# A chunked RWKV-6 recurrence with a squared-ReLU MLP behind it: the chunk decay moved beside the state update, one cumulative sum from step 5 on, a last tile in two column halves, and a new order of work

## The chip, the cores and the metric

The kernel runs on one core of one Trainium2 chip. The metric is the device time of one execution in microseconds (us). Lower is better. Six runs of the kernel before took 197.55 to 198.88 us, with a median of 198.63 us.

Five engines work at once, each through its own list of instructions in order: TensorE (PE in the profile; its weight loads are PEld), VectorE (DVE), ScalarE (ACT), GpSimd (POOL) and SyncE (SP), which issues all DMA transfers here. TensorE writes only to PSUM, a memory of eight banks, and VectorE or ScalarE read it from there.

## The reference

There are 4 batches, 8 heads, 768 positions and a head width of 48. First a recurrence runs over the positions, once for each batch and head:

```python
for t in range(S):
    cur = einsum('bhd,bhe->bhde', u * k[t], v[t])
    y[t] = einsum('bhd,bhde->bhe', r[t], state + cur)
    state = w[t][..., None] * state + einsum('bhd,bhe->bhde', k[t], v[t])
```

The result is laid out as 3072 tokens of 384 values, x, and goes through two matrices: `h = x @ w_in` (384 to 2048), `g = max(h, 0)**2`, `out = g @ w_out` (2048 to 384). All arrays are float32. The kernel computes the products in bfloat16 with float32 sums.

## The kernel before, in words

**Steps.** A batch's 768 positions are cut into 6 chunks of 128, so there are 24 steps (`NSTEP`), one per batch and chunk, each for all 8 heads at once. Within a chunk the recurrence becomes matrix products. The decay w enters as a logarithm, which is summed along the chunk:

- `lw` (line 154, ScalarE): logarithm of w into one of `NLW = 3` padded buffers.
- `cum` (line 187, PE): sums along the chunk by a product with a triangular matrix into PSUM bank tile `cp`: line 196 without the position itself, for r, and for steps below `V5 = 8` line 198 too, the negated sum with the position itself, for k. In steps whose state is needed later (all but the last chunk of a batch) lines 191 to 195 form in the same bank, in 8 spare columns, the sum over the whole chunk for every head: one matmul that puts -30000 where a column belongs to the other head of a pair, and four matmuls of the logarithms with ones.
- `exp` (line 200, ScalarE): exponentials in place. From step 8 on there is only one sum, and the exponential for k is taken from it with the sign turned (lines 205 and 206). `rw` (ScalarE) and `kw` (GpSimd) then first divide k by w, so that this sum is the right one. Lines 207 to 209 take the exponential of the chunk sums, `a_c`.
- `rd` (line 211, VectorE): r and k times those exponentials, as `rdec`. `tr` (line 217, PE) transposes it with 8 matmuls into bank tile `tr`, `rkt` (VectorE) copies it out, `p` (PE) forms the scores in `cp`, `pm` (VectorE) masks them.
- `su` (line 244, PE): the chunk's own contribution to the state, k^T v, for pairs of heads, in the bank tile `tr` again. `ts` (line 251, VectorE) adds the old state, `sn` (line 259, GpSimd) multiplies by `a_c` and gives the next state.
- `ku`, `qp`, `vq` (GpSimd) and `q` (VectorE) form the term with u. `y` (PE) adds scores times v and r times the state in bank tile `y`, `ysb` (VectorE) adds the u term, `yt` (PE, bank tile `tr`) transposes the sum and `xt` (ScalarE) puts it in x.

The pools behind `cp`, `tr` and `y` (lines 58 to 60) have one buffer each: the next user of such a bank waits until everything that reads it has ended.

**The two layers.** Tokens go in 12 blocks of 256, that is two steps. `m1` (PE, line 300) makes 6 matmuls for 256 of the 2048 columns, and there are 8 such groups in a block. `rl` (ScalarE, line 309) applies the ReLU, `gt` (VectorE, line 317) squares two groups together. `m2` (PE, line 324) multiplies a quarter of the 2048 rows for one half (128 tokens) of the block, 4 matmuls, into one of four banks; after four quarters `os` (ScalarE, line 329) brings the 128 x 384 result to a buffer, and `store` sends it out. The weights arrive as 8 + 8 float32 pieces (`ld:..:I` and `ld:..:O`) and are cast to bfloat16 by `cast`, even pairs on ScalarE and odd pairs on VectorE. A group `m1:i:g` needs piece g of the first matrix, and the quarter q of `m2` the pieces 2q and 2q+1 of the second.

**Fillers.** `warm:n:b` issues n matmuls of 512 columns on zeros. They compute nothing and keep TensorE's clock up while it would wait.

**The order.** All of it is written out by hand in one string, `order`, of 1029 words. `rd:4` is `rd` of step 4, `m2:0:1:2:0` is block 0, half 1, quarter 2, bank 0, and `ld:5:r` is the load of r for step 5. Each engine takes its words in that order and waits at each for its inputs, its buffers and its bank; nothing overtakes. The four loads of a step have 192 KB each, in rows of 192 bytes.

```python
    with tc.manual_schedule(engines={E.PE, E.DVE, E.Activation, E.Pool, E.SP}):
        for word in order.split():
            name, *args = word.split(":")
            run[name](*[int(x) if x.isdigit() else x for x in args])
```

Of the kernel before, what the change touches and what calls it, by code (L numbers as in the profile page):

```python
# [16 lines left out]
def kernel(  # L17
# [15 lines left out]
    C = 128  # L33
# [29 lines left out]
    def bank(b):  # L63
        return ps_mm.tile([C, 512], FP32, name=f"mm{b}")
# [43 lines left out]
    u_row = consts.tile([1, H, D], FP32)  # L108
# [3 lines left out]
    def load_u():  # L112
        nc.sync.dma_start(out=u_row[:], in_=u[None])

    def ub_():
        ps = tiles["ub"] = ps_y_pool.tile([C, H, D], FP32, name="y")
        nc.tensor.matmul(ps[:], ones_row[:], u_row[:], start=True, stop=True)
# [19 lines left out]
    V5 = 8  # L137
    NLW = 3
# [61 lines left out]
    def exp_(s):  # L200
# [6 lines left out]
        if s % NCH < NCH - 1:  # L207
            a_c = tiles["a_c", s] = a_small.tile([C, HP, 2], FP32, name="a_c")
            nc.scalar.activation(a_c[:], cs[:, 0, DM:DM + 2 * HP].rearrange("p (a e) -> p a e", e=2), AF.Exp)  # L209
# [34 lines left out]
    def su_(s):  # L244
        rdec, v_bf = tiles["rdec", s], tiles["v", s]
        ps_su = tiles["su", s] = ps_tr_pool.tile([C, HP, 2, D], FP32, name="tr")
        for p in range(HP):
            nc.tensor.matmul(ps_su[:, p], rdec[:, 1, 2 * p:2 * p + 2, :],  # L248
                             v_bf[:, 2 * p:2 * p + 2, :], start=True, stop=True)

    def ts_(s):
        ps_su = tiles.pop(("su", s))
        ts = tiles["ts", s] = a_mid.tile([C, HP, 2, D], FP32, name="t_state")
        if s % NCH == 0:
            nc.vector.tensor_copy(ts[:], ps_su[:])
        else:
            nc.vector.tensor_add(ts[:], tiles["S", s][:], ps_su[:])  # L257
# [76 lines left out]

    def warm_(n, b):
# [4 lines left out]
    def ld_(n, x):  # L340
        {"i": load_wi, "o": load_wo}.get(x.lower(), lambda g: load_u() if x == "u" else load_step(g, x))(n)

    run = dict(rw=rw_, kw=kw_, lw=lw_, v=v_, cum=cum_, exp=exp_, rd=rd_, tr=tr_, rkt=rkt_, p=p_, pm=pm_, su=su_, ts=ts_,
# [4 lines left out]
        ld:0:w ld:0:r warm:6:0 ld:1:w ld:0:k lw:0 ld:0:u cum:0 ld:0:v warm:4:1 ld:1:v lw:1 ld:1:r exp:0 ub ld:1:k rd:0  # L348
# [103 lines left out]
```

## Time and profile before

| | us |
|---|---|
| median of six runs | 198.63 |
| the profiled execution's own time | 198.88 |
| its span, first to last instruction | 197.1 |
| PE busy | 189.0 (96%) |
| VectorE busy | 145.4 (74%) |
| ScalarE busy | 131.1 (67%) |
| GpSimd busy | 109.1 (55%) |
| share of 16 DMA engines' time used by loads and stores | 66.1% |
| first group of the first layer starts | 26.2 |
| last evacuation (`os`) starts | 193.4 |

The span is cut into 40 slices of 4.93 us in the rows that are shown below, one digit for each: a 9 stands for 90% or more. PEclk is the clock that TensorE was granted, in tenths. A waits row reads: engine and line that waited, what it waited for, total us, how many times, the longest. A chain row reads: start, length, engine, what it wrote, line, how many instructions. Matmul durations in a profile overlap, since they are pipelined, so the distance between two starts says what a group costs.

### The profile page before, as it was taken

The numbers are of one execution on the slowest core, as the hardware profiler recorded it, in microseconds if no ns is written. First come the engines' busy times: TensorE is split into PE (matmuls) and PEld (weight loads), VectorE is DVE, ScalarE is ACT, GpSimd is POOL, SyncE is SP. The second block draws the span as 40 slices with busy tenths as digits, with TensorE's granted clock in tenths as the row PEclk, the third lists the DMA queues.
The fourth block names the chain that finished last, engine by engine and source line by source line (L and its number), as shares of the span: only waits on it lengthen the run. The fifth ranks groups of instructions, "written<-read, shape, count | busy, mean of one in ns | idle before, by whom it ended". The sixth has DMA issues, their size and how long they took to land.

```text
span 197.1 us, 4956 instructions
## 1 busy us (share of the span) xinstructions
PE 189.0 (96%) x1954; PEld 136.7 (69%) x1958; DVE 145.4 (74%) x202; ACT 131.1 (67%) x278; POOL 109.1 (55%) x124
## 2 busy tenths in 40 slices
PE   6899999999899999999999999999999999999992
PEld 2355576776578777678776688877777778778650
DVE  3348997996879979997969876977897885844210
ACT  3615487894689878879974767678776668438221
POOL 6275926026499899693996299430999390010000
PEclk9879999999999999999999999999999999999999
DMA  6999999989999899899998088615730000015013
GB/s 127 216 227 197 299 256 270 327 182 268 211 184 203 196 189 230 171 213 212 228 195 183 3 179 222 141 22 141 151 74 0 3 0 2 3 40 203 0 40 120
DMA packets 108696, 30.20 MB, mean 153 GB/s; under 512 B 100481, under 2 KB 108674, under 8 KB 108674
## 3 DMA queue, kind: packets, MB, share of 16 engines
q1 hardware_dynamic: 108674, 29.89, 66.1%
q8 instruction: 15, 0.25, 0.5%
q14 instruction: 7, 0.06, 0.1%
HBM read 25.17 MB, written 4.72 MB: 152 GB/s over the span
## 4 chain that ended last, share of the span: by engine, by line
PE 79%; DVE 9%; DMA 5%; ACT 2%; issue 2%; SPq 1%; DVEq 0%; ACTq 0%
PE mm L300 27%; PE mm L324 27%; PE tr L222 6%; PE mm L338 4%; PE cp L234 4%; DMA rk_raw<-in_r_dram 3%; DVE gt L317 3%; PE y L269 2%; PE tr L285 2%; PE cp L196 2%; PE tr L248 2%; DMA w_raw<-in_w_dram 2%; DVE rdec_buf L213 2%; PE y L274 2%; DVE pmT L239 1%
## 5 line engine op out<-in xcount | busy, mean ns | idle before, releaser
L300 PE MATMUL mm<-xT,wi_sb 128*128 128x256 bf16 x576 | 72.7, 273 | 0.4 <-DVE wi_sb L104 0.3
L324 PE MATMUL mm<-wo_sb,gt 128*128 128x384 bf16 x384 | 71.6, 326 | 0.0
L309 ACT ACTIVATE rl<-mm 128x512 f16<-128x512 f32 x96 | 55.6, 599 | 19.6 <-PE mm L300 14.8
L300 PEld LDWEIGHTS <-wi_sb 128*128 128x128 bf16 x576 | 54.1, 98 | 10.1 <-DVE wi_sb L104 0.8
L324 PEld LDWEIGHTS <-gt 128*128 128x128 bf16 x384 | 35.8, 98 | 19.0
L317 DVE TENSOR_TENSOR gt<-rl 128x1024 bf16<-128x1024 f16 x48 | 41.6, 883 | 9.7 <-ACT rl L309 9.7
L261 POOL TENSOR_TENSOR S<-t_state,a_c 128x384 bf16<-128x384 f32 x20 | 17.7, 886 | 32.1 <-DVE t_state L257 16.4
L239 DVE TENSOR_TENSOR pmT<-cp,tri_strict 128x1024 bf16<-128x1024 f32 x24 | 29.2, 1219 | 5.7 <-PE cp L234 5.4
L184 POOL TENSOR_TENSOR vq<-v_raw,q 128x384 f32<-128x384 f32 x24 | 22.7, 949 | 16.8 <-DVE q L180 15.4
L172 POOL TENSOR_TENSOR ku<-rk_raw,u_bc 128x384 f32<-128x384 f32 x24 | 25.1, 1048 | 8.3 <-DMA rk_raw<-in_k_dram 4.3
L213 DVE TENSOR_TENSOR rdec_buf<-rk_raw,cp 128x768 bf16<-128x768 f32 x24 | 22.8, 950 | 8.6 <-ACT a_c L209 5.5
L176 POOL TENSOR_TENSOR qprod<-rk_raw,ku 128x384 f32<-128x384 f32 x24 | 25.1, 1050 | 0.5
L226 DVE COPY rkT<-tr 128x1024 bf16<-128x1024 bf16 x24 | 16.5, 688 | 8.8 <-PE tr L222 8.5
L164 POOL TENSOR_TENSOR rk_raw<-rk_raw,rw 128x384 f32<-128x384 f32 x16 | 18.2, 1136 | 5.9 <-ACT rw L160 5.8
L288 ACT COPY xT<-tr 128x384 bf16<-128x384 bf16 x24 | 11.5, 479 | 9.9 <-PE tr L285 9.8
L329 ACT ACTIVATE o_sb<-mm 128x384 f32<-128x384 f32 x24 | 11.6, 491 | 9.7 <-PE mm L324 9.6
L338 PE MATMUL mm<-warm 128*128 128x512 bf16 x52 | 16.5, 435 | 1.5 <-DVE ones L132 1.3
L156 ACT ACTIVATE lw_buf<-w_raw 128x384 bf16<-128x384 f32 x24 | 12.4, 521 | 6.2 <-DMA w_raw<-in_w_dram 6.2
L279 DVE TENSOR_TENSOR y_sb<-vq,y 128x384 bf16<-128x384 f32 x24 | 13.2, 549 | 3.8 <-PE y L274 3.3
L222 PE MATMUL tr<-ident,rdec_buf 128*128 128x128 bf16 x192 | 15.1, 223 | 0.7 <-DVE rdec_buf L213 0.6
L222 PEld LDWEIGHTS <-rdec_buf 128*128 128x128 bf16 x192 | 12.7, 100 | 3.3 <-DVE rdec_buf L213 1.5
L180 DVE TENSOR_REDUCE q<-qprod 128x8 f32<-128x384 f32 x24 | 13.0, 546 | 0.1
(53 smaller groups left out, 179.3 us busy)
## 6 DMA issues: line engine op xcount, KB each, us to landing
w_raw<-in_w_dram SPq DMA_DIRECT2D x24, 192.0 KB, 3.9
rk_raw<-in_r_dram SPq DMA_DIRECT2D x24, 192.0 KB, 3.8
rk_raw<-in_k_dram SPq DMA_DIRECT2D x24, 192.0 KB, 3.8
v_raw<-in_v_dram SPq DMA_DIRECT2D x24, 192.0 KB, 3.8
out_dram<-o_sb SPq DMA_DIRECT2D x24, 192.0 KB, 2.2
w_st<-in_moe_w_in_dram SPq DMA_DIRECT2D x8, 384.0 KB, 5.9
w_st<-in_moe_w_out_dram SPq DMA_DIRECT2D x8, 384.0 KB, 5.6
u_row<-in_u_dram SPq DMA_DIRECT2D x1, 1.5 KB
```

The lines of the kernel that those rows point to most:

```text
L164: nc.gpsimd.tensor_mul(k_s, k_s, tiles.pop(("rw", s))[:])
L172: nc.gpsimd.tensor_mul(ku[:], raw["rk", s][:, 1], u_bc[:])
L176: nc.gpsimd.tensor_mul(qp[:], raw["rk", s][:, 0], tiles.pop(("ku", s))[:])
L184: nc.gpsimd.tensor_mul(vq[:], raw["v", s][:], tiles.pop(("q", s))[:, :, None].to_broadcast([C, H, D]))
L213: nc.vector.tensor_mul(rdec[:, :, :, 0:D], raw["rk", s][:], tiles.pop(("cs", s))[:, :, 0:DM].rearrange("p a (h d) -> p a h d", h=H))
L222: nc.tensor.transpose(ps_tr[:, i, p, :], rdec[:, i, 2 * p:2 * p + 2, :], ident[:])
L239: nc.vector.tensor_mul(pmT[:].rearrange("p e a t -> p (e a) t"), tiles.pop(("p", s))[:].rearrange("p e (a t) -> p (e a) t", a=HP), tri_str ...
L300: nc.tensor.matmul(ps1[:, j * width:(j + 1) * width], wi_sb[:, kk, n * 128:(n + 1) * 128], xT[:, kk, s0 * C:s0 * C + width], start=(kk == ...
L309: nc.scalar.activation(tiles["rl", i, q][:, j], tiles.pop(("m1", i, g))[:], AF.Relu, scale=RS)
L317: nc.vector.tensor_mul(tiles["gt", i][:, 4 * q:4 * q + 4, :].rearrange("p a b -> p (a b)"), rl, rl)
L324: nc.tensor.matmul(tiles["m2", i, mt][:, 0:DM], gt[:, n, mt * 128:(mt + 1) * 128], wo_sb[:, n, :], start=(n == 0), stop=(n == NT - 1))
L338: nc.tensor.matmul(ps[:], warm[:, 0:C], warm[:], start=True, stop=True)
```

## The change

The five matmuls for the chunk sums leave `cum` and follow the state update in `su`, in spare columns of the bank `tr`. A new word, `ac`, takes their exponential there on ScalarE. `V5` becomes 5, so that steps 5, 6 and 7 have one cumulative sum, and get `rw` and `kw`. `NLW` becomes 4. The row of u is loaded into the first row of `u_bc`. A new word, `last`, computes the last 128 tokens of the output as two halves of 192 columns, each with its own bank, evacuation (the first on ScalarE, the second on VectorE) and store. And the whole order is written anew: fillers go from 14 words with 56 matmuls to 16 words with 49, every load is still made once, and the words of each step keep their dependences. Of the order the diff here shows the first rows, to where step 6 is transposed, and the last.

```diff
--- before.py
+++ after.py
@@ -105,16 +105,16 @@
 
     u_bc = consts.tile([C, H, D], FP32)
 
-    u_row = consts.tile([1, H, D], FP32)
+    u_row = u_bc[0:1]
     ones_row = consts.tile([1, C], FP32)
     nc.vector.memset(ones_row[:], 1.0)
 
     def load_u():
-        nc.sync.dma_start(out=u_row[:], in_=u[None])
+        nc.sync.dma_start(out=u_row, in_=u[None])
 
     def ub_():
         ps = tiles["ub"] = ps_y_pool.tile([C, H, D], FP32, name="y")
-        nc.tensor.matmul(ps[:], ones_row[:], u_row[:], start=True, stop=True)
+        nc.tensor.matmul(ps[:], ones_row[:], u_row, start=True, stop=True)
 
     def uc_():
         nc.scalar.copy(u_bc[:], tiles.pop("ub")[:])
@@ -134,8 +134,8 @@
     nc.gpsimd.memset(other_head[:], 0.0)
     nc.gpsimd.memset(other_head[0:DP, :, 1:2], -30000.0)
     nc.gpsimd.memset(other_head[DP:C, :, 0:1], -30000.0)
-    V5 = 8
-    NLW = 3
+    V5 = 5
+    NLW = 4
     lw_bufs = []
     for i in range(NLW):
         t = consts.tile([C, H, DP], BF16, name=f"lw_buf{i}")
@@ -187,12 +187,6 @@
     def cum_(s):
         lw = tiles["lw", s]
         cs = tiles["cs", s] = ps_cp.tile([C, 2, 512], FP32, name="cp")
-        if s % NCH < NCH - 1:
-            nc.tensor.matmul(cs[:, 0, DM:DM + 2 * HP], ident[:], other_head[:], start=True,
-                             stop=False, skip_group_check=True)
-            for p in range(HP):
-                nc.tensor.matmul(cs[:, 0, DM + 2 * p:DM + 2 * p + 2], lw[:, 2 * p:2 * p + 2, :],
-                                 ones2[:], start=False, stop=True, skip_group_check=True)
         nc.tensor.matmul(cs[:, 0, 0:DM], tri_strict[:], lw[:, :, 0:D], start=True, stop=True)
         if s < V5:
             nc.tensor.matmul(cs[:, 1, 0:DM], tri_incl_neg[:], lw[:, :, 0:D], start=True, stop=True)
@@ -204,9 +198,9 @@
         else:
             nc.scalar.activation(cs[:, 1, 0:DM], cs[:, 0, 0:DM], AF.Exp, scale=-1.0)
             nc.scalar.activation(cs[:, 0, 0:DM], cs[:, 0, 0:DM], AF.Exp)
-        if s % NCH < NCH - 1:
-            a_c = tiles["a_c", s] = a_small.tile([C, HP, 2], FP32, name="a_c")
-            nc.scalar.activation(a_c[:], cs[:, 0, DM:DM + 2 * HP].rearrange("p (a e) -> p a e", e=2), AF.Exp)
+    def ac_(s):
+        a_c = tiles["a_c", s] = a_small.tile([C, HP, 2], FP32, name="a_c")
+        nc.scalar.activation(a_c[:], tiles["su", s][:, DM:DM + 2 * HP].rearrange("p (a e) -> p a e", e=2), AF.Exp)
 
     def rd_(s):
         rdec = tiles["rdec", s] = rdec_bufs[s % NRD]
@@ -242,19 +236,24 @@
             tri_strict[:, None, :].to_broadcast([C, 2 * HP, C]))
 
     def su_(s):
-        rdec, v_bf = tiles["rdec", s], tiles["v", s]
-        ps_su = tiles["su", s] = ps_tr_pool.tile([C, HP, 2, D], FP32, name="tr")
+        rdec, v_bf, lw = tiles["rdec", s], tiles["v", s], tiles["lw", s]
+        ps_su = tiles["su", s] = ps_tr_pool.tile([C, 512], FP32, name="tr")
         for p in range(HP):
-            nc.tensor.matmul(ps_su[:, p], rdec[:, 1, 2 * p:2 * p + 2, :],
+            nc.tensor.matmul(ps_su[:, p * 2 * D:(p + 1) * 2 * D], rdec[:, 1, 2 * p:2 * p + 2, :],
                              v_bf[:, 2 * p:2 * p + 2, :], start=True, stop=True)
+        nc.tensor.matmul(ps_su[:, DM:DM + 2 * HP], ident[:], other_head[:], start=True,
+                         stop=False, skip_group_check=True)
+        for p in range(HP):
+            nc.tensor.matmul(ps_su[:, DM + 2 * p:DM + 2 * p + 2], lw[:, 2 * p:2 * p + 2, :],
+                             ones2[:], start=False, stop=True, skip_group_check=True)
 
     def ts_(s):
-        ps_su = tiles.pop(("su", s))
+        ps_su = tiles.pop(("su", s))[:, 0:DM].rearrange("p (a e d) -> p a e d", a=HP, e=2)
         ts = tiles["ts", s] = a_mid.tile([C, HP, 2, D], FP32, name="t_state")
         if s % NCH == 0:
-            nc.vector.tensor_copy(ts[:], ps_su[:])
+            nc.vector.tensor_copy(ts[:], ps_su)
         else:
-            nc.vector.tensor_add(ts[:], tiles["S", s][:], ps_su[:])
+            nc.vector.tensor_add(ts[:], tiles["S", s][:], ps_su)
 
     def sn_(s):
         S = tiles["S", s + 1] = a_mid.tile([C, HP, 2, D], BF16, name="S", bufs=3)
@@ -332,6 +331,19 @@
         t0 = (blocks[i][0] + mt) * C
         nc.sync.dma_start(out=out[t0:t0 + C, :], in_=tiles.pop(("o", i, mt))[:])
 
+    def last_(i, mt, b, j):
+        gt, cols = tiles["gt", i], slice(j * DM // 2, (j + 1) * DM // 2)
+        ps, o_sb = bank(b), o_pool.tile([C, DM], FP32, name="o_sb")
+        for n in range(NT):
+            nc.tensor.matmul(ps[:, 0:DM // 2], gt[:, n, mt * 128:(mt + 1) * 128], wo_sb[:, n, cols],
+                             start=(n == 0), stop=(n == NT - 1))
+        if j == 0:
+            nc.scalar.activation(o_sb[:, cols], ps[:, 0:DM // 2], AF.Copy, scale=1.0 / (RS * RS))
+        else:
+            nc.vector.tensor_scalar_mul(o_sb[:, cols], ps[:, 0:DM // 2], 1.0 / (RS * RS))
+        t0 = (blocks[i][0] + mt) * C
+        nc.sync.dma_start(out=out[t0:t0 + C, cols], in_=o_sb[:, cols])
+
     def warm_(n, b):
         ps = bank(b)
         for _ in range(n):
@@ -340,79 +352,79 @@
     def ld_(n, x):
         {"i": load_wi, "o": load_wo}.get(x.lower(), lambda g: load_u() if x == "u" else load_step(g, x))(n)
 
-    run = dict(rw=rw_, kw=kw_, lw=lw_, v=v_, cum=cum_, exp=exp_, rd=rd_, tr=tr_, rkt=rkt_, p=p_, pm=pm_, su=su_, ts=ts_,
+    run = dict(rw=rw_, kw=kw_, ac=ac_, last=last_, lw=lw_, v=v_, cum=cum_, exp=exp_, rd=rd_, tr=tr_, rkt=rkt_, p=p_, pm=pm_, su=su_, ts=ts_,
                sn=sn_, y=y_, ysb=ysb_, yt=yt_, xt=xt_, ku=ku_, qp=qp_, q=q_, vq=vq_, cast=cast, m1=m1_,
                rl=rl_, gt=gt_, m2=m2_, os=os_, store=store, ld=ld_, warm=warm_, ub=ub_, uc=uc_)
 
     order = """
-        ld:0:w ld:0:r warm:6:0 ld:1:w ld:0:k lw:0 ld:0:u cum:0 ld:0:v warm:4:1 ld:1:v lw:1 ld:1:r exp:0 ub ld:1:k rd:0
-        warm:1:2 uc ld:2:w cum:1 v:0 ku:0 exp:1 su:0 ld:3:w warm:3:3 ts:0 v:1 tr:0 sn:0 ld:2:v warm:9:0 rd:1 ku:1 ld:2:r
-        rkt:0 qp:0 lw:2 ld:2:k p:0 qp:1 tr:1 pm:0 ld:0:I warm:4:1 ld:3:r ld:4:w rkt:1 cum:2 y:0 exp:2 su:1 ld:3:k
-        warm:10:2 ts:1 v:2 q:1 sn:1 rd:2 ku:2 ld:3:v q:0 cast:i:0:0 p:1 su:2 vq:0 pm:1 warm:5:3 lw:3 ld:1:I ld:2:I qp:2
-        ld:3:I ts:2 cum:3 ld:4:I ysb:0 vq:1 tr:2 exp:3 ld:4:r y:1 rkt:2 ku:3 ld:4:v warm:1:0 rd:3 yt:0 warm:3:1 xt:0
-        qp:3 ysb:1 lw:4 tr:3 sn:2 v:3 p:2 rkt:3 warm:2:2 pm:2 yt:1 ld:5:I warm:4:3 xt:1 cast:i:0:1 cast:i:1:0 p:3 ld:6:I
-        y:2 q:2 m1:0:0:0 pm:3 vq:2 ld:4:k cast:i:2:0 m1:0:2:1 su:3 rl:0:0 ld:5:w ysb:2 m1:0:4:2 ts:3 v:4 cum:4 q:3
-        ld:7:I yt:2 rl:0:4 m1:0:1:3 vq:3 exp:4 y:3 ld:0:O sn:3 warm:3:0 ysb:3 ld:1:O xt:2 cast:i:1:1 rl:0:2 ld:2:O yt:3
-        warm:1:2 ld:3:O m1:0:3:0 xt:3 rd:4 ku:4 ld:6:w cast:i:2:1 m1:1:4:2 ld:4:O qp:4 rl:0:1 su:4 ld:5:k m1:1:5:1 lw:5
-        gt:0:0 m1:0:5:3 rl:0:3 ts:4 rl:1:4 m1:1:2:0 gt:0:1 rl:1:5 m1:1:0:2 cast:i:3:1 rl:0:5 tr:4 cast:i:3:0 rl:1:2
-        m1:1:3:1 rkt:4 ld:5:r cast:o:0:1 m1:0:6:3 gt:0:2 p:4 rl:1:3 m1:1:1:0 cast:o:1:0 rl:1:0 m1:1:6:1 pm:4 rl:1:1
-        ld:5:O m1:1:7:2 cast:o:0:0 ld:6:O gt:1:2 y:4 lw:6 ld:7:O m1:0:7:0 gt:1:0 rl:0:6 cum:5 gt:1:1 rl:0:7 ld:6:k
-        m2:0:0:0:3 exp:5 cast:o:1:1 m2:0:1:0:0 ld:6:r q:4 rl:1:6 m2:0:0:1:3 vq:4 rd:5 cast:o:2:0 m2:0:1:1:0 ld:5:v ku:5
-        m2:1:1:0:1 m2:1:1:1:1 gt:0:3 cast:o:2:1 sn:4 tr:5 cum:6 qp:5 rkt:5 m2:0:1:2:0 exp:6 cast:o:3:0 m2:0:0:2:3 ld:7:w
-        cast:o:3:1 rl:1:7 m2:1:1:2:1 ku:6 q:5 ld:6:v m2:0:0:3:3 rd:6 m2:0:1:3:0 ld:7:k os:0:0 ysb:4 vq:5 tr:6 ld:7:r p:5
-        rkt:6 m2:1:0:0:2 qp:6 lw:7 ld:7:v pm:5 yt:4 v:5 m2:1:0:1:2 os:0:1 ld:8:w xt:4 gt:1:3 cum:7 v:6 y:5 q:6 ld:8:k
...
-        m1:11:3:2 m2:10:1:2:1 rl:11:3 m2:11:0:0:3 os:10:0 gt:11:1 m2:10:1:3:1 store:10:0 m2:11:1:0:2 m2:11:0:1:3
-        m2:11:0:2:3 m2:11:0:3:3 m2:11:1:1:2 os:11:0 m2:11:1:2:2 os:10:1 store:10:1 m2:11:1:3:2 store:11:0 os:11:1
-        store:11:1
+        ld:0:w ld:0:r warm:6:0 ld:0:k ld:0:u ld:1:w lw:0 ld:1:r cum:0 warm:2:1 ld:1:k exp:0 ub rd:0 ld:0:v lw:1 ld:0:I
+        ld:2:w cum:1 tr:0 ld:1:v exp:1 warm:8:2 rkt:0 uc ld:3:w rd:1 ku:0 v:0 tr:1 ku:1 p:0 rkt:1 warm:2:3 ld:2:v qp:0
+        pm:0 su:0 warm:3:0 ld:2:r ac:0 qp:1 ts:0 v:1 p:1 ld:2:k y:0 lw:2 q:0 su:1 sn:0 warm:6:1 cast:i:0:0 ld:3:k pm:1
+        vq:0 ac:1 ld:3:r q:1 cum:2 warm:5:2 ysb:0 exp:2 vq:1 ld:1:I ld:2:I ts:1 v:2 ld:4:w rd:2 yt:0 sn:1 y:1 lw:3
+        warm:1:3 xt:0 ld:3:v ku:2 ysb:1 cum:3 su:2 warm:4:0 ac:2 qp:2 ld:3:I exp:3 ts:2 yt:1 warm:2:1 rd:3 ku:3 xt:1
+        ld:5:w tr:2 cast:i:0:1 m1:0:0:2 ld:4:I sn:2 rkt:2 cast:i:1:0 warm:1:3 ld:4:r q:2 p:2 lw:4 m1:0:1:0 pm:2 vq:2 v:3
+        tr:3 ld:5:I rl:0:0 qp:3 warm:1:1 rl:0:1 rkt:3 y:2 ld:4:k cast:i:1:1 su:3 lw:5 m1:0:2:3 ysb:2 ld:6:I ac:3 rw:5
+        m1:0:3:1 q:3 ld:5:k p:3 ts:3 vq:3 cast:i:2:0 pm:3 yt:2 warm:1:2 sn:3 ld:7:I rl:0:2 m1:0:4:0 xt:2 gt:0:0 y:3
+        ld:4:v rl:0:3 cum:4 ysb:3 warm:2:2 exp:4 ku:4 yt:3 ld:5:r warm:4:3 xt:3 cast:i:2:1 qp:4 rl:0:4 ld:0:O rd:4
+        m1:0:5:1 ld:1:O ku:5 rl:0:5 cum:5 ld:5:v m1:1:0:2 exp:5 gt:0:1 m1:1:2:3 ld:2:O kw:5 q:4 m1:1:1:0 rl:1:0 ld:3:O
+        gt:0:2 cast:i:3:0 tr:4 ld:4:O vq:4 m1:1:4:1 rd:5 ld:6:w rl:1:1 qp:5 m1:1:6:2 v:4 rkt:4 m1:0:6:0 rl:1:4
+        cast:i:3:1 p:4 rl:1:6 su:4 gt:1:0 ld:6:k m1:1:7:1 cast:o:0:0 pm:4 m1:0:7:2 rl:1:7 ld:5:O ac:4 m1:1:5:1 gt:1:3
+        rl:0:6 ld:6:O y:4 rl:0:7 ts:4 warm:1:0 cast:o:0:1 rl:1:2 tr:5 ld:7:O q:5 v:5 m2:1:1:0:0 cast:o:1:0 rkt:5 ld:7:w
+        vq:5 m2:0:1:0:2 ysb:4 rl:1:5 p:5 ld:7:k cast:o:1:1 yt:4 lw:6 m1:1:3:3 ku:6 pm:5 xt:4 ld:6:r m2:0:1:1:2 rw:6 sn:4
+        m2:0:0:0:1 cast:o:2:0 cum:6 cast:o:2:1 y:5 exp:6 kw:6 m2:0:0:1:1 ysb:5 m2:0:0:2:1 cast:o:3:0 gt:0:3 ld:8:w yt:5
+        m2:0:1:2:2 cast:o:3:1 rl:1:3 ld:7:r gt:1:2 m2:0:0:3:1 xt:5 lw:7 m2:0:1:3:2 ku:7 ld:8:k os:0:0 m1:2:2:3 rw:7 rd:6
+        qp:6 ld:6:v m1:2:3:1 os:0:1 lw:8 gt:1:1 cum:7 ld:8:r tr:6 kw:7 exp:7 m1:2:4:2 rkt:6 ld:7:v m2:1:1:1:0 qp:7 rw:8
...
+        m2:10:1:0:0 rl:11:0 m1:11:1:3 rl:11:2 m1:11:3:2 m2:10:0:0:1 rl:11:3 m2:10:1:1:0 rl:11:1 gt:11:1 m2:10:1:2:0
+        gt:11:3 m2:10:0:1:1 gt:11:0 m2:10:0:2:1 m2:10:1:3:0 m2:10:0:3:1 os:10:1 m2:11:0:0:2 os:10:0 m2:11:0:1:2
+        m2:11:0:2:2 m2:11:0:3:2 os:11:0 store:11:0 store:10:1 store:9:1 store:10:0 last:11:1:3:0 last:11:1:0:1
```

## The prediction, made before the change was run

> **What bounds the kernel now.** I read the page first: busy shares, the forty slices, the waits.
>
> ```profile
> PE 189.0 (96%) x1954; PEld 136.7 (69%) x1958; DVE 145.4 (74%) x202; ACT 131.1 (67%) x278; POOL 109.1 (55%) x124
> PE   6899999999899999999999999999999999999992
> PEclk9879999999999999999999999999999999999999
> DMA  6999999989999899899998088615730000015013
> ```
>
> TensorE (PE) is busy throughout and next to nothing else is idle for it. But the DMA row is full too, for about the first 100 us, so in that stretch data can set the pace. Busy time doesn't separate these, so I took the distance between the starts of neighbouring PE groups, and the chain that ended last shows the same lengths:
>
> ```profile
> 50.59 0.62 PE tr L222 x8
> ...
> 68.11 0.45 PE tr L222 x8
> 68.56 0.65 PE mm L300 x6
> 69.21 0.65 PE mm L324 x4
> ```
>
> Undisturbed, a first-layer group (L300, x6) costs 0.655, a second-layer group (L324, x4) 0.650, a transpose group (L222, x8) 0.447, scores (L234, x8) 0.330, an output group (L269+L274) 0.372 or 0.204 without state, a state update (L248, x4) 0.170, a decay group (L191 + 4 of L194) 0.127, one cumulative sum (L196 or L198) 0.163, a y transpose (L285, x3) 0.167, the u broadcast 0.84. Sum of needed work: 96x0.655 + 96x0.650 + 24x0.447 + 24x0.330 + 20x0.372 + 4x0.204 + 20x0.170 + 20x0.127 + 32x0.163 + 24x0.167 + 0.84 = 168.2 us. The last matmul starts near 193.2, so about 25.0 us of PE time are lost: warm-up fillers and waits. "Lost" at a moment = clock minus needed work issued so far; it never falls. It stands at 18.7 when the first L300 group starts (26.21), 20.3 at 31.80, 20.75 from 38 to 49, 21.55 when `tr:6` starts (50.59), 22.0 at 58, 25.0 at the end. So three quarters is gone before the first-layer work, and the last large step is this one:
>
> ```profile
> 43.74 5.71 DMA rk_raw<-in_r_dram
> 49.57 0.97 DVE rdec_buf L213
> 50.59 0.62 PE tr L222 x8
> ```
>
> The r rows of step 6 land at 49.45, `rd:6` takes 0.97 behind them, and `tr:6` is released. Data are the limit there. The 3.45 us lost later are many small pieces, some 1.6 of it 0.1 at each of sixteen switches to the 64-row score matmuls.
>
> **What the Trainium skill says.** "DMA: Bandwidth & Descriptors", Specifications, wants 512 B or more per transfer for line rate; step loads have 192 B rows. The trace agrees: a 192 B packet takes 15.5 ns and a 1536 B one 72.6, that is 12 against 21 B per ns; by the trace's landing marks a step load (192 KB) costs 0.96 us (17 landings from 47.68 to 64.04), a first-layer weight piece (384 KB) about 1.6 and a second-layer piece 1.24. "PSUM — Partial Sum Buffer", PSUM bank collisions raise a hardware error, tells to guard by bank, two readers on different engines included. The trace agrees: rdec waits for the a_c exponential although it doesn't use it, only because both read bank cp:
>
> ```profile
> DVE rdec_buf L213 <- ACT a_c L209: 5.5, 2, 4.3
> ```
>
> "TensorE: Matmul & The Clock Gate", The HAM clock gate, halves the clock after an idle window of about 3.4 us. Here the granted clock is 0.9 from 3 to 20 us and full afterwards; none of the waits that I find below is that long.
>
> **The change, part by part.**
>
> *Decay sums moved to the state update.* The 5 matmuls (0.127) stay, 20 times; PE work is unchanged. In front of rdec goes the 0.178 us exponential and 0.127 of PE: about 0.3 us off a step's chain, hidden behind other PE work except at the start. Added: `ts` now shares its bank with `ac` and comes after it in the order, so VectorE (in order: then gt, rd, rkt) waits for ScalarE's place in its queue, and bank tr comes free later. The next user of bank tr stands at least 1.9 us of PE work behind the state update from step 3 on (0.2 to 4 before), and the ScalarE work ahead of `ac` is nearly all fed by matmuls before the update: cost 0. If ScalarE lags by 1 us, each update costs 0 to 0.5: bound 0 to +4 us.
>
> *One cumulative sum from step 5.* Three L198 matmuls go: -0.49 us. Added: 3 rw (0.525) and three second exponentials (0.48+0.48 against 0.80) on ScalarE, 2.1 us, and 3 k divisions (1.136) on GpSimd, 3.4 us, between 25 and 55 us. A stretch of that time (columns: stretch, its length, busy PE, PEld, DVE, ACT, POOL, clock, DMA share, GB/s):
>
> ```profile
> 36.00:44.00 8.00, 8.00 (x84) 6.12 (x82) 7.88 (x13) 7.20 (x13) 1.09 (x2) 1.00 0.94 251
> ```
>
> GpSimd has the room; ScalarE has 0.8 of 8 us, and VectorE nearly none. Cost on the path 0, because PE waits for data in that stretch anyway; without that cover up to +1.
>
> *Four lw buffers, u in u_bc.* One memset more (0.53) on GpSimd before 5 us, where its first multiply waits 3.8 us anyway: 0.
>
> *Last tile in halves.* 32 matmuls of 192 columns replace 16 of 384. An L324 matmul of 384 columns takes 0.163, one of L300 with 256 columns 0.109, both 0.425 ns per column; at that rate 32x192 columns cost 2.6, as 16x384 do. The evacuation at the end is half as wide, on VectorE: 0.55 for 384 columns (the t_state row), so some 0.35, against 0.49 on ScalarE: -0.14. The last store has half the bytes: eight packets per engine at 72.6 ns were 0.58 us, so -0.25 at most; but four full stores stand right ahead in SP's order behind `os:11:0`, which ends 2.1 us before the last matmul, and stores spaced 0.5 apart in this trace still landed within 2.1 to 2.15. The last then issues at about +0.42 and lands near +2.1, against +2.36 now. Together -0.3 (0 to -0.5).
>
> *Order, the start.* I walk each engine's queue with the durations above, an operation starting when its inputs, its bank and its engine are free. Loads land about 0.95 apart from 3.6 on: k0 5.4, w1 6.4, v0 9.1. `exp:0` no longer sits behind `lw:1`: it starts with cum:0's end, 5.1 instead of 6.12. Then rd:0 6.0 to 6.9 (0.95), cum:1 behind lw:1 and bank cp 7.05, tr:0 7.5, rkt:0 8.1 to 8.8, rd:1 to 9.75, and after eight fillers tr:1 at 9.8 (13.91 before). p:0 10.4, pm:0 11.2 to 12.4, which frees cp for p:1, y:0 12.9. VectorE then runs ts:0, q:0, pm:1, q:1, ysb:0, ts:1, rd:2 back to back until 17.4 (0.55 each, 1.22, 0.95), y:1 is at 16.8, ysb:1 ends 18.0, ts:2 18.9, yt:1 19.0, xt:1 19.3 to 19.8, tr:2, and the first L300 group starts near 20.3 instead of 26.21. But the weight pieces land as late as before (about 27, 29.5, 32, 34.5 for the fifth to eighth), so PE takes a group now and then: by m1:0:5 (31.6 after cast i:2:1 on ScalarE, 12.0 us of work issued) lost is 19.5, against 20.3. The fillers fall from 56 to 49, which is part of this same 0.8.
>
> *Order, 36 to 54 us.* Here I follow SP's queue. r of step 5 is the 23rd step load, behind eight weight pieces: eight pieces and 21 step loads had landed at 34.86, so it lands at 36.7. `rd:5` stands in front of `rkt:4` on VectorE and holds it: 36.7 + 0.95 + 0.69 gives rkt:4 at 38.4, and PE's `p:4` (17.2 us of work) waits for it: lost 21.2. Behind rkt:4 queue cast i:3:1, gt:1:0, pm:4, gt:1:3, ts:4 (0.94+0.69+1.22+0.69+0.55), which release y:4 and tr:5: lost 22.3 at 42.5. The last second-layer piece comes after 26 step loads (24 before, landing 47.68): 49.6, its cast 0.55, so m2:0:0:3 (27.0) starts at 50.2: lost 23.1. r of step 6 comes after v5, w7 and k7, which it used to precede: 49.45 + 3x0.96 = 52.3; rd:6 until 53.3; tr:6 (29.8 us of work) at 53.4: lost 23.6 against 21.55, **+2.0 us**. Bounds: the DMA share fell to 0.79 from 42 to 46; if the new order closes that gap, 0.8 less; a cast one ScalarE slot late adds 0.6. After that the order has slack: step loads from 7 on arrive 0.8 us or more before PE asks, and from step 9 over 2 us. The later 3.45 I keep (2 to 4.5).
>
> Sum against the profiled execution: +2.0 - 0.5 - 0.3 = +1.2, span 197.1 to 198.3. That execution's time was 198.88, 1.8 outside its span; the median of the runs is 198.63, so I predict 198.63 + 1.2 = 199.8.
>
> **Rivals.** *Faster, 197.1:* the early lead of 0.8 holds, and r6 is not the limit; with -0.5 and -0.3 that is -1.6. For it: tr:1 four us earlier, seven fillers fewer. It decides if r6 lands before about 50.5, two step loads sooner than I count. Against it: the DMA is full to 40 us in both orders. *No change, 198.6:* the DMA gap at 42 to 46 closes (-0.8) and later small waits shrink by 0.5, since state updates have more room in bank tr. For it: the waits ahead of y:8 and tr:10 cost 0.4 together today, that ahead of p:12 0.3. *Worse, 201.8:* ac holds bank tr and VectorE; 20 updates at 0.1 to 0.15 us add 2 to the +1.2. It decides from a ScalarE lag of 2 us behind the matmuls. Against it: in the ten-microsecond stretches after 100 us ScalarE is busy 4.0 to 8.1 of 10. That the decay move does nothing for PE is part of my sum.
>
> **Numbers.** Forecast 0.55, its own range 199.3 to 201.0; worse 0.12; no change 0.20; faster 0.13. A measurement of this kernel can tell about 0.3% (0.6 us) from no change. Slower 0.67, same 0.20, faster 0.13. The range 198.2 to 201.6 leaves out most of the faster case and half of the worse.
>
> **What would show it.** First L300 group at 20 to 21.5; a VectorE wait of some 2 us for r of step 5 near 36.7 and p:4 at 38.4; tr:6 near 53.4 behind `rd:6` and a DMA landing near 52.3; then PE dense to about 194.6; GpSimd busy 3.9 us more and ScalarE 1.9; the last store landing within 2.2 us of the last matmul. I am wrong if tr:6 starts before 51.7, or if ts waits on ac pile up after 60 us.

## The result, and the profile after

The changed kernel takes 200.39 us (median of 29 runs), beside 198.73 us for the kernel before (66 runs). The ratio is 1.0065, with a 95% interval from 1.0046 to 1.0083: 1.3 us slower (0.0065 x 198.7). A ratio here counts only the executions within 1.5% of the quickest of the same kernel (20 of 30 for the changed kernel), so where this matters the text also gives the ratio of the means of all executions, which is 1.0079 for the changed kernel (1.6 us, with an error of 0.4). The prediction was 199.8, in the range 198.2 to 201.6. The profiled execution is one of the quicker ones: 199.48 us, span 197.5, against 198.88 and 197.1 before.

The page of the kernel after, with the busy times and the slices that answer to those shown of before (it has no row for the clock, since this trace holds no record of it):

```profile
PE 185.9 (94%) x1960; PEld 135.9 (69%) x1964; DVE 145.2 (74%) x203; ACT 131.6 (67%) x284; POOL 111.7 (57%) x128
...
PE   7896888988899999999999999999999999999993
DMA  6998999989999999999929972495300100203005
```

PE has work of 167.7 us instead of 168.2, is busy 3.1 us less (fewer fillers, and faster ones, see the last section), and ends later: the last matmul ends at 194.5, 193.3 before. Behind its first slice the DMA row stands at 8 or 9 tenths to about 99 us (20 slices of 4.94 us), as it did before.

The chain that ended last, of the kernel after, answers to the one shown of before (start, length, what):

```profile
51.95 0.96 DVE rdec_buf L207
52.91 0.04 issue
52.95 0.32 PE cp L190
53.28 0.45 PE tr L216 x8
53.72 0.65 PE mm L299 x6
```

The r rows of step 6 were issued at 46.63 and landed 5.2 us later, at 51.83 (49.45 before):

```profile
46.63 2.43 SPq L67 DMA_DIRECT2D rk_raw<-in_r_dram  x1
```

```profile
rk_raw<-in_r_dram SPq DMA_DIRECT2D x1, 192.0 KB, 5.2
```

The product with the decay started 0.12 us after that, as it did in `before`, `r6_late` and `r6_early`, where the profile names these rows as what ended its wait, and PE's next cumulative sum and transpose waited for its end. Here the profile names an evacuation on ScalarE instead:

```profile
DVE rdec_buf L207 <- ACT o_sb L328: 1.5, 1, 1.5
```

That evacuation ended at 51.85, next to the landing, but the product does not use it. The late rows are the step on which the prediction put 2.0 us.

I use the prediction's "lost" again: the time in the trace minus the needed PE work issued so far. One row per trace, at five amounts of issued work; 8 us is about where the first L299/L300 group starts, 14 is past the group `m1:0:5` (after) or `m1:0:3` (before), 30 past `tr:6`:

```
                  8       14      30      36      end of PE
before          18.67   20.33   21.66   21.94   25.16
r6_late         17.60   20.51   24.19   24.48   27.22
tail_alone      17.66   19.58   20.75   21.04   24.58
few_before      17.60   19.27   19.47   19.76   22.49
tail_decay      18.05   20.45   21.37   21.67   28.40
after           15.82   20.02   23.31   23.40   26.77
r6_early        16.41   20.35   21.43   22.17   25.75
r6_sn4          16.54   21.12   22.89   23.67   27.00
r6_cast         15.95   19.39   23.77   24.53   28.05
v5_back         15.94   20.08   23.65   23.76   26.65
few_after       16.22   20.17   21.55   21.64   23.98
decay_back      17.46   21.70   25.17   25.37   29.57
decay_back2     15.52   20.22   23.59   23.80   27.12
```

The last two rows are one and the same kernel: single executions differ by up to 2.5 us, so a row shows where time goes, and the timed ratios say how much. In the two rows that matter most, `before` and `after`: the new order is 2.85 us ahead at 8 (1.6 just behind it, since a wait of 1.2 us follows there), 0.3 ahead at 14, and 1.65 behind at 30. From there to the end both lose the same, 3.46 and 3.50.

### The profile page after: what moved, and what is told of

Read it like the earlier page. It is cut to its first block, busy times and chain, and to the rows that moved or that the text cites. A ratio compares the mean times of both kernels' runs of the same rounds, so it can differ in the third digit from the quotient of the medians.

```text
span 197.5 us, 4952 instructions
## 1 busy us (share of the span) xinstructions
PE 185.9 (94%) x1960; PEld 135.9 (69%) x1964; DVE 145.2 (74%) x203; ACT 131.6 (67%) x284; POOL 111.7 (57%) x128
## 4 chain that ended last, share of the span: by engine, by line
PE 61%; SPq 13%; DMA 9%; DVE 6%; ACT 5%; issue 4%; DVEq 0%; ACTq 0%
PE mm L299 24%; PE mm L323 23%; SPq L67 10%; DMA w_raw<-in_w_dram 4%; PE tr L216 3%; DMA w_st<-in_moe_w_in_dram 3%; PE cp L228 2%; DMA v_raw<-in_v_dram 2%; ACT rl L308 2%; PE cp L190 2%; PE y L268 2%; SPq L332 1%; PE tr L284 1%; PE mm L338 1%; DVE pmT L233 1%
## 5 line engine op out<-in xcount | busy, mean ns | idle before, releaser
L299 PE MATMUL mm<-xT,wi_sb 128*128 128x256 bf16 x576 | 74.0, 273 | 0.9 <-ACT wi_sb L104 0.4
L323 PE MATMUL mm<-wo_sb,gt 128*128 128x384 bf16 x368 | 70.1, 326 | 0.0
L299 PEld LDWEIGHTS <-wi_sb 128*128 128x128 bf16 x576 | 53.7, 98 | 11.2 <-ACT wi_sb L104 1.3
L323 PEld LDWEIGHTS <-gt 128*128 128x128 bf16 x368 | 33.9, 98 | 17.9 <-issue 0.8
L172 POOL TENSOR_TENSOR ku<-rk_raw,u_bc 128x384 f32<-128x384 f32 x24 | 24.2, 1011 | 13.7 <-DMA rk_raw<-in_k_dram 9.1
L184 POOL TENSOR_TENSOR vq<-v_raw,q 128x384 f32<-128x384 f32 x24 | 21.5, 903 | 18.4 <-DVE q L180 18.4
L176 POOL TENSOR_TENSOR qprod<-rk_raw,ku 128x384 f32<-128x384 f32 x24 | 26.2, 1095 | 3.3 <-DMA rk_raw<-in_r_dram 2.8
L164 POOL TENSOR_TENSOR rk_raw<-rk_raw,rw 128x384 f32<-128x384 f32 x19 | 21.5, 1132 | 11.3 <-ACT rw L160 10.5
L168 ACT CAST v_bf<-v_raw 128x384 bf16<-128x384 f32 x24 | 12.3, 512 | 3.9 <-DMA v_raw<-in_v_dram 3.8
L350 PE MATMUL mm<-warm 128*128 128x512 bf16 x45 | 13.5, 416 | 1.4 <-DVE warm L129 1.3
L216 PE MATMUL tr<-ident,rdec_buf 128*128 128x128 bf16 x192 | 14.6, 219 | 0.1
```

Source lines behind the costliest of these rows:

```text
L164: nc.gpsimd.tensor_mul(k_s, k_s, tiles.pop(("rw", s))[:])
L172: nc.gpsimd.tensor_mul(ku[:], raw["rk", s][:, 1], u_bc[:])
L176: nc.gpsimd.tensor_mul(qp[:], raw["rk", s][:, 0], tiles.pop(("ku", s))[:])
L184: nc.gpsimd.tensor_mul(vq[:], raw["v", s][:], tiles.pop(("q", s))[:, :, None].to_broadcast([C, H, D]))
L216: nc.tensor.transpose(ps_tr[:, i, p, :], rdec[:, i, 2 * p:2 * p + 2, :], ident[:])
L299: nc.tensor.matmul(ps1[:, j * width:(j + 1) * width], wi_sb[:, kk, n * 128:(n + 1) * 128], xT[:, kk, s0 * C:s0 * C + width], start=(kk == ...
```

## The experiments

### Late r rows in the kernel before, and few weight loads in both

In `r6_late` the kernel before loads the r rows of step 6 three places later, and nothing else is changed:

```diff
-... m2:0:1:0:0 ld:6:r q:4 ...
+... m2:0:1:0:0 q:4 ...
-... ld:6:v m2:0:0:3:3 ...
+... ld:6:v ld:6:r m2:0:0:3:3 ...
```

> The kernel before with one word moved: the load of r for step 6 goes behind three other step loads (v5, w7, v6) on SP. If data set the pace there, r6 lands some 2.9 us later (near 52.3), the transpose of step 6 starts near 53.4 instead of 50.59, and the time grows by 2.4 to 2.8 us, to about 201.2. If PE has other work to hide it, or the wait is absorbed later, it grows by less than 0.5.

Measured: ratio to before 1.0158 (1.0112 to 1.0203), 3.1 us slower. The chain of this run:

```profile
48.30 3.69 DMA rk_raw<-in_r_dram
...
52.11 0.97 DVE rdec_buf L213
...
53.12 0.62 PE tr L222 x8
```

`tr:6` starts at 53.1, as in the changed kernel, and lost goes from 21.2 to 24.2 there. So this one load, in this place, sets the pace of PE in the old order. The 3.1 us agree, within the interval, with the 2.4 to 2.8 that the data theory asked for.

In `few_before` and `few_after` 14 of the 16 weight pieces are not loaded, and all casts read the first piece of their matrix, so that the output is that of other weights, while the work of PE, VectorE, ScalarE and GpSimd stays the same.

```diff
     def load_wi(h):
+        if h:
+            return
     def load_wo(h):
+        if h:
+            return
-        copy(dst, w_st.pop((kind, h))[:])
+        copy(dst, w_st[kind, 0][:])
```

> The kernel before, with 14 of the 16 weight pieces not loaded (every cast reads the first piece of its matrix, so the two layers compute with wrong weights); all casts and matmuls stay. It takes some 20 us of DMA time away before 50 us. Theory (data set the pace up to 54 us): the wait for r6 and the filler time near 30 us go, 1 to 2 us less than before, 197.2. It is the base for its counterpart.

> The changed kernel with the same 14 weight pieces not loaded. Theory: its loss lies in data that come late in the first 54 us, so without it it is no longer slower: 0.5 to 1.5 us faster than the kernel before with the same loads left out, some 196. Rival (ScalarE's decay exponential holds bank tr and VectorE, or the added ScalarE and GpSimd work): it stays 1 us or more slower than that one.

Measured, against before: 0.9886 (0.9842 to 0.993) and 0.9918 (0.988 to 0.9957). `few_before` is 2.3 us faster than the kernel before, where 1 to 2 were expected. `few_before` loses 0.2 us between 14 and 30 instead of 1.3: PE's waits in that stretch were for data. `few_after` loses 1.4 there instead of 3.3, so some 1.9 us of what the changed kernel lost there was late data as well. But the kernel before loses 1.1 us there to late data too. So of the 2.0 us that the new order loses more than the old one between 14 and 30, the pair of traces puts 0.8 down to late data, and 1.2 stay, 0.6 of them where a second-layer group waits for VectorE's squares (at 48.44 in `few_after`).

I had expected `few_after` to be 0.5 to 1.5 us faster than `few_before`, and it is not: at 0.9918 over 0.9886 it is 0.6 us slower, with an error of 1.2. The rival, that the order costs 1 us or more without late data too, is therefore not excluded. And the early lead, 1.4 us at 8, has become 0.9 us behind by 14, with hardly a weight load in the way, so late weights are not what eats the lead.

The largest part of what eats it stands in the timeline of the changed kernel (start, length, engine, work, and the idle time before it with what ended it):

```profile
30.76 0.48 ACT L287 COPY xT<-tr 128x384 bf16<-128x384 bf16 x1
31.14 0.83 ACT L104 CAST wi_sb<-w_st 128x768 bf16<-128x768 f32 x1
```

```profile
30.56 1.03 PE L350 MATMUL mm<-warm 128*128 128x512 bf16 x4
32.03 0.83 PE L299 MATMUL mm<-xT,wi_sb 128*128 128x256 bf16 x6 [0.44 <-ACT wi_sb L104]
```

The cast that `m1:0:5` needs is queued on ScalarE behind the exponential of step 4 and the copy of y of step 3, though its piece landed at 29.6; and four fillers stand in front of `m1:0:5`. Together 1.48 us are lost there, and 1.46 in `few_after`. That is 1.5 of the 4.2 us that the changed kernel loses between 8 and 14. Another 1.2 go right behind 8, where the output group of step 2 waits for its masked scores, which VectorE makes behind a weight cast; the rest are smaller waits and fillers.

### The loads, a state and a cast put earlier in the changed kernel

```diff
 r6_early
-... ld:7:k ... ld:6:r ... ku:7 ... qp:6 ...
+... ld:6:r ld:7:k ... qp:6 ku:7 ...
 r6_sn4, on top of r6_early
-... ku:6 ... sn:4 ...
+... sn:4 ku:6 ...
 r6_cast, on top of r6_early
-... exp:4 ... xt:3 cast:i:2:1 ...
+... cast:i:2:1 exp:4 ... xt:3 ...
```

`r6_early` takes the product `qp:6`, which needs these rows, ahead of `ku:7` on GpSimd too.

> The changed kernel with the r rows of step 6 loaded one place earlier (ahead of k of step 7). Data theory: r of step 6 lands near 51.1 instead of 51.95, its product with the decay no longer holds the cumulative sum of step 7, and the 0.76 us lost there goes: 0.5 to 0.8 us faster than the changed kernel, ratio to before 1.0025 to 1.004. Rival, engine order: the wait moves to the next thing on PE and nothing is gained, ratio 1.0065.

Measured: 1.0035 (1.0004 to 1.0066), 0.6 us faster than the changed kernel with an error of 0.7. The means of all executions give 1.0074 (error 0.003), beside 1.0079. So the gain that the data theory asked for is not shown by the times. In the trace VectorE takes the product when the rows are there, at 49.61, and PE no longer waits at `tr:6`:

```profile
49.61 0.95 DVE L207 TENSOR_TENSOR rdec_buf<-rk_raw,cp 128x768 bf16<-128x768 f32 x1 [0.27 <-DMA rk_raw<-in_r_dram]
```

That is earlier than the 51.1 expected, because all loads came earlier in this execution (the last second-layer piece at 48.15 instead of 49.28).

`r6_sn4` goes for a wait that the prediction did not have. In the changed kernel the output group of step 5 stood for 0.71 us for the state, which GpSimd made late, since the bonus product of step 6 stands ahead of it in GpSimd's order and waits for k rows (landing 45.27):

```profile
45.34 1.00 POOL L172 TENSOR_TENSOR ku<-rk_raw,u_bc 128x384 f32<-128x384 f32 x1 [3.06 <-DMA rk_raw<-in_k_dram]
46.29 0.83 POOL L260 TENSOR_TENSOR S<-t_state,a_c 128x384 bf16<-128x384 f32 x1
```

```profile
47.18 0.33 PE L273 MATMUL y<-S,rkT 128*128 128x96 bf16 x4 [0.71 <-POOL S L260]
```

> As the run before, and the new state of step 4 is computed on GpSimd ahead of the bonus product of step 6, which waits for k of step 6. Data theory: the 0.87 us wait of the output group of step 5 goes, but the last second-layer piece, which lands near 49.4 and is cast by 50.0, holds PE to the same clock: 0.5 to 1.0 us faster than the changed kernel, ratio 1.0015 to 1.004, no more than 0.3 better than the run before. Rival, the two waits are independent: both sums come in, 1.6 us faster, ratio 0.9985.

Measured: 1.005 (1.0012 to 1.0089). The wait is gone from the trace (lost does not move between 23 and 27 us of work), and the time is no better than that of `r6_early` (over all executions 1.0073, beside 1.0074). The rival's 0.9985 is outside the interval. So taking away this PE wait, which stood ahead of a later wait for data, bought nothing that can be measured here.

> The changed kernel with the r rows of step 6 loaded one place earlier (alone: ratio 1.0035), and the cast of the sixth first-layer piece on ScalarE ahead of the exponential of step 4 instead of behind the copy of y of step 3. Engine-order theory: m1:0:5 starts near 30.9 instead of 32.0 to 32.4, so the 1.48 us lost there shrinks to 0.2 to 0.5. Data theory for the rest: the scores of step 4 and m2:0:0:3 stand where r of step 5 and the last second-layer piece land, so next to nothing of it is left by 50 us: ratio 1.002 to 1.0045. Rival: the gain is kept to the end, 1.0 to 1.3 us, ratio 0.997 to 0.9985.

Measured: 0.9998 (0.9964 to 1.0032), which looks as if the two moves together took back the loss. But this rests on 8 of 22 executions. The means of all, 199.42 and 198.05 us, give 1.0069 (error 0.003), beside 1.0079 for the changed kernel: 0.2 us, with an error of 0.7. So no gain is shown. The smaller ratio touches both expected ranges; that of all executions lies above both, nearer to the data theory's. In its trace, an execution of 200.81 us, the cast is ready at 30.2 and `m1:0:5` starts at 31.41, not 30.9: what is left, 0.86, are the four fillers. The 0.6 won there is gone by the end of the second layer's first block, where `m2:0:0:3` and `m2:0:1:3` wait for the last two second-layer pieces (lost grows by 1.85; the cast of the last piece starts at 50.51).

### The tail alone

```diff
-... m2:11:1:0:2 ... m2:11:1:3:2 ... os:11:1 store:11:1
+... last:11:1:2:0 last:11:1:0:1
```

This is put into the kernel before, with the new function `last_`; the rest is as it was.

> The kernel before with only the last 128 tokens in two column halves; its stores stay where they were. Theory of the prediction: 0.3 us less (0 to 0.5). If the two traces are right, in which 3.7 us lay between the last matmul and the end before and 3.0 after, 0.7 less: 198.0.

Measured: 0.9987 (0.9965 to 1.0009), 0.26 us faster, which can't be told from nothing. From the last matmul's end to the landing of the last store it is 2.05 us in its trace, 2.39 before and 2.06 in the changed kernel; to the span's end 3.46, 3.74 and 3.04. The last evacuation and stores of the changed kernel are

```profile
194.27 0.94 SPq L345 DMA_DIRECT2D out_dram<-o_sb  x2
194.50 0.36 DVE L343 TENSOR_SCALAR o_sb<-mm 128x192 f32<-128x192 f32 x1 [7.27 <-PE mm L338]
```

The 0.36 was forecast as 0.35.

### One cumulative sum undone

```diff
-    V5 = 5
+    V5 = 8
-... rw:5 ... kw:5 ... rw:6 ... kw:6 ... rw:7 ... kw:7 ...
```

> The changed kernel with two cumulative sums again for steps 5 to 7, and without their ScalarE and GpSimd work. Prediction's step: the three matmuls cost 0.49 us, but those of steps 5 and 6 stand where PE waits for data, so 0.16 to 0.5 us slower than the changed kernel, ratio 1.007 to 1.009. Rival: the ScalarE and GpSimd work of the one-sum form costs more in that stretch than the matmuls save, and undoing it gives 0.5 to 1 us: ratio 1.0015 to 1.004.

Measured: 1.0054 (1.0032 to 1.0077), 0.2 us faster than the changed kernel, with an error of 0.6 (over all executions 1.0058, beside 1.0079). Neither the gain that the prediction counted nor a cost shows. PE has 0.49 us more to do and ends at 194.83 instead of 194.46, in one execution of each.

### The decay sums, in both orders

`decay_back` is the changed kernel with the sums and their exponential back in the bank of the cumulative sum; `decay_back2` is the same kernel again.

```diff
     def su_(s):
-        nc.tensor.matmul(ps_su[:, DM:DM + 2 * HP], ident[:], other_head[:], ...)
-        for p in range(HP):
-            nc.tensor.matmul(ps_su[:, DM + 2 * p:DM + 2 * p + 2], lw[:, 2 * p:2 * p + 2, :], ones2[:], ...)
     def cum_(s):
+        if s % NCH < NCH - 1:
+            ... the same five matmuls, into cs[:, 0, ...]
-... su:0 ... ac:0 ...
+... exp:0 ac:0 ... su:0 ...
```

> The changed kernel with the decay sums and their exponential back beside the cumulative sum (its bank, its place). Prediction's theory: the move costs and gains nothing, so within 0.6 us of the changed kernel, ratio 1.0035 to 1.0095. Rival a: the new wait of VectorE's state sum for the decay exponential costs PE time, and undoing it gives 0.6 us or more, ratio under 1.0035. Rival b: the move pays, since it takes 0.3 us off each step's chain, and undoing it costs 0.6 us or more, ratio over 1.0095.

> A second measurement of the changed kernel with the decay sums back beside the cumulative sum. If undoing the move costs time: ratio 1.010 to 1.016 again, and in the trace the r and k product waits for the decay exponential in at least four steps. If the first measurement was chance: ratio 1.005 to 1.009, within the changed kernel's own interval.

Measured: 1.0132 (1.0079 to 1.0184) in 6 runs, then 1.0079 (1.0054 to 1.0104) in 22. The first was mostly chance. Weighted by their errors they give about 1.009, so undoing the move costs 0.5 us, with an error of 0.6: in the new order it is worth 0 to 1 us, which is no more than the error.

`tail_decay` makes the same move in the kernel before, in its own order, together with the tail in halves: 20 times the decay exponential `ac:s` comes right ahead of `ts:s`, with its sums in `su_`. Since the sums now read the logarithms later, it has five log buffers, and two words of step 19 stand further back; the row of u sits in `u_bc`, as in the change. `old_order` made the move too, with four log buffers, `ac:s` right behind `su:s`, the one-sum form for steps 5 to 7 and the tail in halves; my placing of its words spoiled it.

```diff
-    NLW = 3
+    NLW = 5
-... su:14 ... ts:14 ...
+... su:14 lw:19 rw:19 ... ac:14 ts:14 ...
```

The words of `old_order`, for one of the steps:

```diff
-... lw:7 ... rd:7 ... ku:7 ... su:7 ... ts:7 ...
+... lw:7 rw:7 ... ku:7 kw:7 rd:7 ... su:7 ac:7 ... ts:7 ...
```

> All code of the change (decay sums beside the state update, one cumulative sum from step 5 on, four buffers, last tile in halves) in the engine order of before; only the words that the code needs are put in, next to their neighbours. Prediction's theory: the loss lies in the order alone, so tail 0.3 and one-sum 0.2 to 0.5 come in: 0.5 to 0.8 us faster than before, ratio 0.996 to 0.9975. Rival: the code itself costs (ScalarE and GpSimd work in a stretch where they have little room, the state sum behind the decay exponential), ratio over 1.001.

> The kernel before in its own order, with the last tile in halves (alone: ratio 0.9987) and the decay sums moved to the state update, their exponential right ahead of the state sum in the list; five lw buffers, and the logarithm of step 19 moved behind the state update of step 14, since the sums read it later. Prediction's theory, the move is worth nothing: ratio 0.9975 to 1.0005. Rival, the move pays wherever it is made, as undoing it in the changed kernel cost 1.3 us: ratio 0.992 to 0.996.

Measured: `old_order` 1.0324 (1.0277 to 1.0371), `tail_decay` 1.0144 (1.0093 to 1.0195). In `old_order` four log buffers are too few, so that the sums of steps 14 and 15 read the logs of steps 18 and 19; and GpSimd, with `ku:7` and `kw:7` behind `vq:6`, held `rd:7` for nearly 2.0 us. So it says little of the change itself. It does show what the place right behind the state update costs: ScalarE waited there 14.6 us, in 17 waits.

`tail_decay` is the telling one. With the tail alone at 0.9987, the move costs 3.1 us here (0.0157 x 198.7), with an error of about 1.1. Up to 36 us of work it runs like the kernel before, and then loses 6.7 us to the end instead of 3.2. The waits of `tail_decay`:

```profile
DVE t_state L256 <- ACT a_c L203: 8.9, 11, 1.8
...
DVE t_state L254 <- ACT a_c L203: 5.3, 3, 2.2
...
PE tr L216 <- DVE t_state L256: 1.4, 3, 0.8
...
PE tr L216 <- DVE t_state L254: 0.9, 2, 0.6
```

And of the changed kernel:

```profile
ACT a_c L203 <- PE tr L247: 5.8, 7, 2.3
...
DVE t_state L256 <- ACT a_c L203: 2.8, 4, 1.6
```

The state sum shares its bank with the decay exponential and waits for ScalarE: 14.2 us in 14 waits in the old order, 2.8 us in 4 in the new. While it waits, VectorE does nothing else and the bank stays taken, so the next transpose is late, for instance at `tr:12` and `tr:16`:

```profile
94.21 0.56 DVE L254 COPY t_state<-tr 128x384 f32<-128x384 f32 x1 [1.54 <-ACT a_c L203]
...
116.58 0.55 DVE L256 TENSOR_TENSOR t_state<-S,tr 128x384 f32<-128x384 bf16 x1 [1.85 <-ACT a_c L203]
```

The second is in part my own doing: the logarithm of step 19, moved behind `su:14`, stands ahead of that exponential on ScalarE. PE lost 0.96 there; the other 2 us or so have nothing to do with it. So the mechanism of the rival "worse" is real. In the new order it hardly acts; that this comes from the room behind each update, and not from the place of the exponential in ScalarE's list, is argued and was not tested apart.

## Why the prediction was right, and where its steps were not

**The late r rows (+2.0).** Right in place and time: `tr:6` was to start at 53.4 with 23.6 lost, behind rows landing near 52.3. It started at 53.1, lost stood at 23.3, and the rows landed at 51.83. `r6_late` shows that rows as late as this cost the kernel before 3.1 us.

How much of the changed kernel's loss they are is not shown. By the trace PE lost 0.76 us there, of which the profile shows 0.60 as idle time:

```profile
52.95 0.32 PE L190 MATMUL cp<-lw_buf,tri_strict 128*128 128x384 bf16 x1 [0.60 <-DVE rdec_buf L207]
```

The kernel before lost 0.80 for its own rows of step 6. When these waits began, the new order was already 1.8 us behind (lost 22.54 beside 20.74). Most of that had gone between 43 and 48 us, at the scores and the output group of step 5; had PE come sooner, it would have waited longer for the rows. So two limits lie close together, and taking away one of them (`r6_early`, `r6_sn4`) gave no gain clear of the scatter.

**The start.** The first L299 group was to start near 20.3, and started at 21.44. The chain of small steps kept to the forecast up to `y:0` (12.4, forecast 12.9). Then VectorE stood still 1.9 us for the k rows of step 2, which landed at 17.28:

```profile
17.40 0.95 DVE L207 TENSOR_TENSOR rdec_buf<-rk_raw,cp 128x768 bf16<-128x768 f32 x1 [1.92 <-DMA rk_raw<-in_k_dram]
```

The prediction had VectorE busy without a break there. The lead was to shrink to 0.8 by `m1:0:5` because of late weights. It shrank to 0.3, and the largest single cause was another: the cast behind two other ScalarE operations, and four fillers. The prediction had that cast ending at 31.6 "on ScalarE" (it ended at 31.97), but ascribed the loss to the weights; `few_after` shows it with hardly a weight load left.

**The scores of step 4 (lost 21.2).** This step failed in the profiled execution. r of step 5 was counted to land at 36.7 and landed at 35.57, so `p:4` started at 37.3 with 20.1 lost. In the other traces of this order it was in part seen: r of step 5 landed between 34.74 and 38.08, and 0.25 to 0.8 us were lost at `p:4` in five of them. The wait is there when the rows land later than in the profiled execution, or when PE comes sooner (`r6_cast`), so my count of landings was at the late end of what happens.

**A wait not foreseen.** The output group of step 5 behind GpSimd's queue lost 0.87 in lost time between 46 and 47. It made up for the missing loss at `p:4`, and had no effect of its own that `r6_sn4` could show.

**The three matmuls (-0.5).** This term should not have been in the sum at full size. The prediction itself says that PE waits for data in that stretch; then matmuls taken out of it only make the wait longer. `v5_back` finds no gain. The added work off PE was too high in the forecast as well: GpSimd is busy 2.6 us more than before instead of 3.9, ScalarE 0.5 instead of 1.9. On paper the forecast's lost time was 0.3 too large and gave a part of that back.

**The tail (-0.3).** 0.26 alone. By the landing of the last store it is about 0.33, in both traces of the halves that are compared above. Right in size, below what the timing can tell.

**The decay move (0, with a bound of +4).** 0 to -1 in the new order; in the old one it costs 3.1 us. The prediction argued the value from the order (at least 1.9 us of PE work between the update and the bank's next user), and the two orders agree with that; the bound of +4 is where the old order went.

**Later losses (3.45 kept).** 3.46 by the table.

So the sum of 1.2 against the measured 1.3 is in part luck, since errors cancel: the gain of the one-sum was not there, and the data cost a little less than counted. What stays open is how the 1.3 us divide. Neither earlier r rows nor an earlier cast with them give back anything that all their executions show (0.1 and 0.2 us, errors 0.7), and with few weight loads the two orders can't be told apart. That late r rows in this place cost time is shown in the old order; that they are what the new order loses is argued from its trace. Of the kernels that do all the work none is clearly faster than the kernel before; the tail in halves, in the old order, comes closest with 0.26 us.

## What to carry to other kernels

While the transfers set the pace, compare the two orders by the position of each load in the one queue, and look for the engine that waits for the load that comes last; here savings on PE (`v5_back`) and a wait removed ahead of it (`r6_sn4`) bought nothing that could be measured. Before a reader is added to a bank, ask what stands between its engine's place in the order and the other reader: the same five matmuls and one small exponential cost nothing in one order and 3 us in another. And where executions scatter by 1% and more, read places from a trace, but sizes from many runs, and from all of them: `r6_cast` stood at 0.9998 by a third of its executions and stands at 1.0069 by all.

## What the runs showed of the hardware that was not expected

TensorE came to its full speed at different moments of the start. Transposes and fillers in the same place, first of the changed kernel, then of `decay_back`:

```profile
7.30 0.61 PE L216 MATMUL tr<-ident,rdec_buf 128*128 128x128 bf16 x8
7.75 1.89 PE L350 MATMUL mm<-warm 128*128 128x512 bf16 x8
```

```profile
8.33 1.06 PE L222 MATMUL tr<-ident,rdec_buf 128*128 128x128 bf16 x8
9.19 3.62 PE L351 MATMUL mm<-warm 128*128 128x512 bf16 x8
12.60 1.06 PE L222 MATMUL tr<-ident,rdec_buf 128*128 128x128 bf16 x8
```

A filler takes 0.236 us in one and 0.45 in the other. The record of the granted clock in the trace of `decay_back` begins only at 13.62 us, with full clock; the row of its page reads 9 in every slice, since that row takes a time without a record as full. `decay_back2`, the same kernel, has its first record, and full speed, at 5.67. Of 14 traces three, that of before among them, ran at half speed somewhere between 8 and 13 us. So the length of a known filler is a better witness than the row.

The Trainium skill, "TensorE: Matmul & The Clock Gate", Part 1: The HAM clock gate, says that the moment varies from run to run, since the activity window doesn't start with the kernel; these traces agree, and by more than the half microsecond that it names: where a record stands, full clock begins between 4.46 and 13.62 us. It also says that about 3.4 us of steady work bring full speed; in `decay_back` PE worked from 1.3 us on with gaps under 0.3 us, and needed over 12.

The clock of the kernel before was full from 5.18 us, 0.50 from 8.59 to 12.01 and full again, with no gap on PE above 0.9 us ahead of it. The 0.9 that the prediction read for 3 to 20 us is a mean over this, and the idle window of about 3.4 us that it names was not needed there. After the work the clock turns to 0.5 between 2.0 and 5.2 us behind the last matmul, in each of the 13 traces that have a record. No run leaves the fillers out, so what they are worth is not shown.

What the half speed costs can't be read from these traces: the trace of before, with half speed, had lost 20.3 at `m1:0:3`, that of `r6_late`, without it, 20.5.

The loads scatter too: r of step 5 landed at 38.08 and 35.76, r of step 6 at 53.79 and 52.22 in the two executions of the same kernel, `decay_back` and `decay_back2`.
